# A linear-attention and GEGLU block on one core: 1/den from four copies in DRAM, rows summed beside den, and the down projection's first product of each pair moved up

## The chip, the cores and the metric

The kernel runs on one core of one Trainium2 chip. The metric is the device time of one execution in microseconds (us); the kernel before took 783.16 us (median of three runs, 782.22 to 784.1). The engines of a core run their own instruction streams in order and wait for each other through semaphores: PE (matrix multiply, with PEld for its weight loads), DVE (VectorE), ACT (ScalarE), POOL (GpSimd), and SP, which here only issues DMAs.

## The reference

One sequence of 2048 tokens, D = 1024, 32 heads of 32, F = 3584. Six modulation vectors come from `silu(c) @ w_mod`.

```python
h = _layernorm(x, axis=-1) * (1 + ca) + sa
x = x + ga * _A_ref(h, A_wqkv, A_wo)
h = _layernorm(x, axis=-1) * (1 + cb) + sb
x = x + gb * _B_ref(h, B_w_gate, B_w_up, B_w_down)
# _A_ref: linear attention
pq, pk = (phi(q), phi(k))
kv = jnp.einsum('bhsd,bhse->bhde', pk, v)
z = jnp.einsum('bhsd->bhd', pk)
num = jnp.einsum('bhqd,bhde->bhqe', pq, kv)
den = jnp.einsum('bhqd,bhd->bhq', pq, z)[..., None] + 1e-06
o = num / den          # then o @ wo
# _B_ref: gelu(x @ w_gate) * (x @ w_up) @ w_down
```

## The kernel before

The program is built as one list of operations per engine. Each operation names the bytes that it reads and writes; a tracker derives the semaphore waits. From the first attention evictions to the second FFN unit (`mark[0]` to `mark[1]`) a planner, `reorder`, sorts the operations of DVE, ACT and POOL by table costs and due times; PE and SP keep the order in which the code emits them. Everything later is in the written order on all engines. SP issues its DMAs in order, so a DMA that waits holds those behind it; eight DMA lanes limit how many are open.

**Attention (about 30 to 241 us).** K and Q come first. Then 24 `m` tiles (line 895) form pk-transpose times x, four groups `g` with three column parts `k` first, then the rest. Each is evicted by ACT (`mcp`), and a finished group is transposed by a DMA (`mT0` to `mT7`, line 703) and multiplied with wv (`kv`, line 913), whose masked blocks DVE writes to `kvt`. `w2_pair(i)` (line 1201) multiplies two groups of `kvt` with wo in 64x64 array tiles, copied to `w2` by ACT or DVE. The table `HOOK` says which of these follow which tile on PE:

```python
HOOK = {0: "ga", 6: "kv0", 10: "kv1", 11: "w0", 13: "kv2", 15: "modp kv3 z32", 16: "den0", 17: "w1 rb0.0 rb0.1", 18: "",
        19: "kv4", 20: "den1 ps0.0", 21: "gbr", 22: "ps0.1", 23: "rb2.0"}
```

`den(p)` (line 1240) needs `z32`. It forms the denominators of two of the four 512-token groups in 128x32 array tiles (32 matmuls of 256 columns, four at a time). DVE adds 1e-6 and takes the reciprocal into `rdc`, whose 128 partitions are token group, half, and head within a group. A DMA stores `rdc` to DRAM (`scr_rd`, line 1248). `rb_load` (line 1260) reads it back so that partition 32k to 32k+31 of the tile `rb` hold the row of head k: four DMAs for each half of a token group, each of 32 partitions with one 8 KB row. `pq_scale` (line 1273, `pqs`) multiplies pq by it, four DVE operations for a half, each waiting for all four loads. `wo` chunks (line 1283) then give the attention output, and `x1` (line 1291) adds it to x.

The modulation sums (`macc` on DVE) end in rows that are split in a high and a low part and summed over partitions by `mod_rows` (`modr`, line 840, 128x32 array tiles, 8 matmuls): "ga" behind tile 0, the pass for sb and cb ("modp") behind tile 15, the pass for gb ("gbr") behind tile 21. ACT copies the row (`mrow`), a DMA stores it, and `sbT` and `cbT` (line 1230) load it back, 4 bytes at a time.

**FFN (241 to 603 us).** 28 units; each forms two 128-column blocks of gate and up by a scheme of seven block products P1 to P7 in place of eight. P1 and P2 are in bf16, the other five are of sums and in f32.

**Down projection (from 603 us).** Eight pairs of 128-token chunks, the same seven products of 14 matmuls each (`d_prod`, line 1672); the pairs alternate between PSUM banks 0 to 3 and 4 to 7 (`b0`). P1 goes to bank b0, is copied to b0+2 (`dpcp`, ACT), P2 is added in b0. P5 goes to b0+3 and is copied to the SBUF tile `de` (`descp`, ACT). P6 and P7 are added in b0+2; with `de` DVE makes bank b0+1 after P6 and b0+3 after P7 (`dpadd`). P3 is added in b0+1, P4 in b0+2. Each of the four banks is evicted by two DVE operations (`x2a`, `x2b`, lines 1576 and 1577) with the residual tile `xq` and stored (`out`). A pair's operands are loaded from DRAM in two halves (`ya`, line 1571): half 0 serves P1, half 1 P2; DVE makes the sums `dssum0` to `dssum3` of them (line 1648) in two buffers used in turn, ACT a copy (`dscp`, line 1643). `y_next(r)` asks for the next pair's half r, `x_in` (line 1568) for `xq`. The order in a pair is

```python
for k in (1, 5, 6, 2, 7, 3, 4):
```

## Time and profile before

| | |
|---|---|
| median of three runs | 783.16 us (782.22 to 784.1) |
| profiled execution, span from first to last instruction | 780.9 us (780.946); its own time beside the span is not shown |
| mean granted clock of PE | 1.000 |
| PE busy | 770.2 us, 99% |
| DVE busy | 645.9 us, 83% |
| ACT busy | 374.6 us, 48% |
| loads of `rb` | 32 of 256 KB, median 6.0 us from issue to landing |
| DVE's waits for `rb` | 2.2 us in 2 waits |
| PE, 125 to 241 us / 241 to 603 / 603 to 623 / 623 to 778 | busy 115.58 of 116 / 360.06 of 362 / 19.93 of 20 / 154.28 of 155 |

PE's busy time is modelled: matmuls overlap each other, a 512-column matmul is shown as 379 to 398 ns and the next one starts some 216 to 230 ns after it. So 99% does not mean that PE runs at its peak; the distance from one start to the next is what to read. In the timeline a row is a group of like instructions, with the start, the busy time, and the number after x. "PEld" rows are the weight loads, one for each matmul; "SPq" rows are DMA issues on SP's queue. "128*32" in a PE row is the array tile.

### The profile page before, as it was taken

How to read it: one execution, taken by the hardware profiler on the slowest of the kernel's cores; microseconds unless marked ns; L12 is line 12 of the kernel's file. 1: busy time of each engine (PE TensorE's matmuls, PEld its weight loads, DVE VectorE, ACT ScalarE, POOL GpSimd, SP SyncE). 2: the span in 40 equal slices, each digit the busy share in tenths (PEclk: the TensorE clock that was granted, in tenths of full speed). 3: DMA queues.
4: the chain of work that ended last, by engine and by line, in shares of the span. 5: the costliest groups of instructions: out<-in, count | busy, mean ns of one | idle time of the engine just before them, and what ended most of it. 6: DMA issues, size and time to landing. Idle time of an engine off the chain costs nothing.

```text
span 780.9 us, 10753 instructions
## 1 busy us (share of the span) xinstructions
PE 770.2 (99%) x3825; PEld 496.2 (64%) x3883; DVE 645.9 (83%) x964; ACT 374.6 (48%) x629; POOL 47.5 (6%) x126
## 2 busy tenths in 40 slices
PE   8999999999999999999999999999999999999998
PEld 4444445666445667667676767667676576677766
DVE  6699988897899878787989888888989888676767
ACT  2497743242466487878755555555555211111111
POOL 2031300000321011100000000000000000000000
PEclk9999999999999999999999999999999999999999
DMA  9879749939999358867353865535356334443331
GB/s 284 256 167 252 158 91 215 255 80 196 203 287 231 82 138 212 230 175 215 99 145 108 250 211 172 148 96 161 97 147 221 111 127 139 144 141 114 126 125 60
DMA packets 196940, 130.22 MB, mean 167 GB/s; under 512 B 69516, under 2 KB 182420, under 8 KB 195864
## 3 DMA queue, kind: packets, MB, share of 16 engines
q1 hardware_dynamic: 196872, 129.55, 62.4%
q8 instruction: 30, 0.49, 0.3%
q14 instruction: 22, 0.18, 0.1%
q10 hardware_dynamic: 16, 0.00, 0.0%
HBM read 92.55 MB, written 23.35 MB: 148 GB/s over the span
## 4 chain that ended last, share of the span: by engine, by line
PE 95%; SPq 2%; DMA 1%; DVE 1%; issue 1%; ACT 0%; DVEq 0%; ACTq 0%
PE ps_all L1458 45%; PE ps_all L1672 21%; PE ps_all L895 7%; PE ps_all L934 7%; PE ps_all L1283 7%; PE ps_all L880 5%; PE ps_all L1593 1%; SPq L598 1%; DMA wmq<-in_w_mod_dram 1%; SPq L603 1%; DMA h1T<-xh 0%; PE ps_all L913 0%; PE ps_all L1201 0%; PE ps_all L1240 0%; DVE h1T L724 0%
## 5 line engine op out<-in xcount | busy, mean ns | idle before, releaser
L1458 PE MATMUL ps_all<-ss,tp 128*128 128x512 f32 x896 | 214.3, 396 | 0.0
L1458 PEld LDWEIGHTS ps_all<-ss,tp 128*128 128x128 f32 x896 | 168.3, 188 | 37.8 <-DVE ss L1413 0.2
L1672 PE MATMUL ps_all<-dt,sb 128*128 128x512 f32 x424 | 102.5, 398 | 0.0
L1481 ACT ACTIVATE ge<-ps_all 128x512 f32<-128x512 f32 x112 | 64.1, 597 | 73.8 <-DVE ps_all L1469 62.1
L1458 PE MATMUL ps_all<-h2a,wt 128*128 128x512 bf16 x421 | 95.7, 379 | 1.8
L1672 PEld LDWEIGHTS ps_all<-dt,sb 128*128 128x128 f32 x424 | 79.6, 188 | 18.5 <-DVE sb L1648 0.3
L1476 DVE TENSOR_TENSOR ps_all<-ps_all,es 128x512 f32<-128x512 f32 x54 | 37.6, 699 | 49.4 <-ACT es L1466 49.0
L1488 DVE TENSOR_TENSOR ys<-ge,ps_all 128x512 bf16<-128x512 f32 x112 | 74.4, 684 | 3.8 <-PE ps_all L1672 0.5
L1458 PEld LDWEIGHTS ps_all<-h2a,wt 128*128 128x128 bf16 x448 | 38.0, 98 | 57.3 <-ACT ps_all L1463 16.9
L1433 DVE TENSOR_TENSOR tp<-wt 128x1024 fp32r<-128x1024 bf16 x56 | 68.1, 1217 | 1.8 <-DMA wt<-in_B_w_up_dram 1.8
L1433 DVE TENSOR_TENSOR tp<-wt,tp 128x1024 fp32r<-128x1024 bf16 x56 | 68.2, 1218 | 0.0
L934 PE MATMUL ps_all<-h1T,wq 128*128 128x512 bf16 x256 | 56.7, 379 | 0.0
L880 PE MATMUL ps_all<-wk,h1T 128*128 128x512 bf16 x239 | 55.3, 379 | 1.1 <-DMA wk<-in_A_wqkv_dram 0.5
L1283 PE MATMUL ps_all<-w,pq 128*128 128x512 bf16 x249 | 55.7, 379 | 0.5 <-issue 0.2
L1458 PE MATMUL ps_all<-ar,tp 128*128 128x512 f32 x224 | 55.5, 390 | 0.0
L869 ACT ACTIVATE eb<-ps_all 128x512 f32<-128x512 f32 x64 | 36.3, 594 | 37.6 <-PE ps_all L880 16.0
L1672 PE MATMUL ps_all<-wd,ya 128*128 128x512 bf16 x199 | 47.5, 380 | 0.7
L1458 PEld LDWEIGHTS ps_all<-ar,tp 128*128 128x128 f32 x224 | 42.1, 188 | 8.9
L1463 ACT ACTIVATE ps_all<-ps_all 128x512 f32<-128x512 f32 x56 | 32.6, 582 | 26.8 <-PE ps_all L1458 26.5
L934 PEld LDWEIGHTS ps_all<-h1T,wq 128*128 128x128 bf16 x256 | 25.0, 98 | 30.0
L1283 PEld LDWEIGHTS ps_all<-w,pq 128*128 128x128 bf16 x256 | 24.6, 98 | 30.3 <-issue 1.1
L1643 ACT ACTIVATE sb<-ya 128x896 fp32r<-128x896 bf16 (+1 forms) x16 | 14.5, 913 | 58.8 <-PE ps_all L1672 58.8
(141 smaller groups left out, 976.3 us busy)
## 6 DMA issues: line engine op xcount, KB each, us to landing
wt<-in_B_w_gate_dram SPq DMA_DIRECT2D x28, 512.0 KB, 4.0
wt<-in_B_w_up_dram SPq DMA_DIRECT2D x28, 512.0 KB, 5.2
scr_y<-ys SPq DMA_DIRECT2D x28, 512.0 KB, 3.2
ya<-scr_y SPq DMA_DIRECT2D x14, 896.0 KB, 4.9
rb<-scr_rd SPq DMA_DIRECT2D x32, 256.0 KB, 6.0
wd<-in_B_w_down_dram SPq DMA_DIRECT2D x7, 1024.0 KB, 7.6
wmst<-in_w_mod_dram SPq DMA_DIRECT2D x6, 1024.0 KB, 6.2
wmq<-in_w_mod_dram SPq DMA_DIRECT2D x8, 512.0 KB, 7.5
```

What stands on the lines that cost most here:

```text
L869: sch.op(A, lambda e: e.activation(EB[i][:, :], PS(bank), ACTF.Exp), prd=pr(bank), wr=rng, note=f"{note}.exp")
L880: o = sch.op(T, lambda e, dc=dc: e.matmul(PS(bank), H1[sg][:, ci, dc, :], W_[:, dc, jg * 512:(jg + 1) * 512], start=(dc == 0), stop=(dc == ...
L895: o = sch.op(T, lambda e, c_=c_: e.matmul(PS(bank, 0, n), PK[c_][:, g * P:(g + 1) * P], xrow(c_, o_, o_ + n), start=(c_ == 0), stop=(c_ == ...
L934: o = sch.op(T, lambda e, dc=dc: e.matmul(PS(b), WQ[:, dc, qc * P:(qc + 1) * P], H1[sg][:, :, dc, :], start=(dc == 0), stop=(dc == NDC - 1 ...
L1283: last[half] = sch.op(T, lambda e, g=g, half=half: e.matmul(PS(b0 + half), PQ[sg][:, g, ci * P:(ci + 1) * P], W2[:, g, half * 512:(half + ...
L1433: sch.op(V, lambda e: e.tensor_tensor(TP[k][:], in0, in1 if k in (0, 2) else in1[:], ALU.subtract), rd=r0 + r1, wr=r_tp(k), deps=[x1_ops[7 ...
L1458: o = sch.op(T, lambda e, l_=l_, r_=r_, dc=dc: e.matmul(PS(b), l_, r_, start=fresh and dc == 0, stop=dc == ND2 - 1, skip_group_check=True) ...
L1463: sch.op(A, lambda e: e.activation(PS(BB + t), PS(BA + t), ACTF.Copy), prd=pr(BA + t), pwr=pr(BB + t), note="pcp")
L1476: sch.op(V, lambda e: e.tensor_tensor(PS(BC + t), PS(BC + t), ES[t][:, :], ALU.add), prd=pr(BC + t), rd=r_2k(OFF_ES[t], f"es{t}"), pwr=pr( ...
L1481: sch.op(A, lambda e: e.activation(GE[i][:, :], PS(b), ACTF.Gelu_apprx_tanh), prd=pr(b), wr=r_2k(OFF_GE[i], f"ge{i}"), note="gelu")
L1488: sch.op(V, lambda e: e.tensor_tensor(YS[s_][:, 2 * h:2 * h + 2, t, :], q(GE[i][:, :]), q(PS(b + 1)), ALU.mult), rd=r_2k(OFF_GE[i], f"ge{i ...
L1672: o = sch.op(T, lambda e, l_=l_, r_=r_, j=j, dst=dst: e.matmul(dst, l_[:, 0, :], r_, start=(k in (1, 5) or own is not None) and j == js[0] ...
```

## The change

- `scr_rd` gets four copies (`NRP`), so `rdc` is stored four times. `rb_load` still makes four DMAs for a half, but each now fills two of the eight groups on all 128 partitions, rows of 2 KB; every copy serves eight partitions of a head. A `pqs` operation waits for its own load alone. Two dependencies are put in by hand for the planner: the first `pqs` behind the second reciprocal, `pqs2.0` behind the copy `w2cp7`.
- Hooks: "modp" moves from tile 15 to 16, ahead of `den0`, its bank from 5 to 2; `den0` uses bank 3; `w1` moves from 17 to 16, behind `den0`. The stores of `rdc` become hooks of their own (`st0`, `st1`). "gbr" moves from tile 21 to 20, behind `den1`, into bank 6. `sbT` and `cbT` are loaded behind `st1` ("sbl"). On SP's queue `mT4` now stands ahead of the first store, and `mrow2` and `mT6` ahead of the second.
- Down projection, pairs 1 to 6: the order becomes 5, 6, 7, 2, then P1 of the next pair (`d_open`), 3, 4. P1 of pair 1 is opened before the loop. P7 gets bank b0+3 for itself once P5 has been copied from it; `d_join` copies P7 to `de` and adds it to b0+1 (giving b0+3) and to b0+2. Half 1 of `ya` is asked for behind P2, and the `xq` loads are spread differently. The last pair keeps the old order without its P1.

```diff
-    scr_rd = nc.dram_tensor("scr_rd", [NSG, 2, HPG, NG, SGW // 2], f32).ap()
+    NRP = 4
+    scr_rd = nc.dram_tensor("scr_rd", [NSG, 2, HPG, NRP, NG, SGW // 2], f32).ap()
...
-            mod_rows(((0, 2, 5, lambda j, h: (HLG[:, j, h, :], r_hlg(j, h))),))
+            mod_rows(((0, 2, 6, lambda j, h: (HLG[:, j, h, :], r_hlg(j, h))),))
...
-            mod_rows(((2, 4, 5, hl_src),))
-            o_r = mod_store(4, 5, MROW[1], r_2k(OFF_ROW + 2048, "mrow1"), 1)
+            mod_rows(((2, 4, 2, hl_src),))
+            o_sc[0] = mod_store(4, 2, MROW[1], r_2k(OFF_ROW + 2048, "mrow1"), 1)
+
+        o_sc = [None]
+
+        def mod_load():
             for dst, nt, a0 in ((SBT, "sbT", 0), (CBT, "cbT", 2)):
...
-                o_rd[pr_] = sch.dma(Q, lambda e: e.dma_start(scr_rd[2 * pr_:2 * pr_ + 2].rearrange("s f k g t -> (s f k g) t"), RDC[:, :]),
-                          rd=r_sm("rdc"), note=f"rden{pr_}.st")
+                o_rd[pr_] = [sch.dma(Q, lambda e, r=r: e.dma_start(scr_rd[2 * pr_:2 * pr_ + 2, :, :, r, :, :].rearrange("s f k g t -> (s f k) g t"), RDC[:, :]),
+                                     rd=r_sm("rdc"), note=f"rden{pr_}.st") for r in range(NRP)]
...
-                for k in range(HPG):
-                    made.append(sch.dma(Q, lambda e, h=h, k=k: e.dma_start(
-                        RB[i][32 * k:32 * (k + 1), h, :, :].rearrange("p a b -> p (a b)"),
-                        scr_rd[sg, h, k:k + 1, :, :].rearrange("k g t -> k (g t)").to_broadcast([32, NG * HW])),
-                        wr=r_rb(i, h) if k == 0 else (), deps=made[0].deps if k else [o_rd[sg // 2]], note=f"rb{sg}.{h}.{k}"))
+                for g0 in range(0, NG, 2):
+                    src = scr_rd[sg, h, :, :, g0:g0 + 2, :].rearrange("k r g t -> (k r) (g t)").unsqueeze(1).to_broadcast([HPG * NRP, P // (HPG * NRP), 2 * HW])
+                    sch.dma(Q, lambda e, h=h, g0=g0, src=src: e.dma_start(
+                        RB[i][:, h, g0:g0 + 2, :].rearrange("p a b -> p (a b)"), src),
+                        wr=r_rb(i, h, g0, g0 + 2), deps=o_rd[sg // 2], note=f"rb{sg}.{h}.{g0}")
...
-        HOOK = {0: "ga", 6: "kv0", 10: "kv1", 11: "w0", 13: "kv2", 15: "modp kv3 z32", 16: "den0", 17: "w1 rb0.0 rb0.1", 18: "",
-                19: "kv4", 20: "den1 ps0.0", 21: "gbr", 22: "ps0.1", 23: "rb2.0"}
+        HOOK = {0: "ga", 6: "kv0", 10: "kv1", 11: "w0", 13: "kv2", 15: "kv3 z32", 16: "modp den0 w1", 17: "st0 rb0.0 rb0.1", 18: "",
+                19: "kv4", 20: "den1 gbr ps0.0", 22: "st1 sbl ps0.1", 23: "rb2.0"}
...
-            b = b0 + {1: 0, 2: 0, 5: 3, 6: 2, 7: 2, 4: 2, 3: 1}[k] if own is None else own
+            b = b0 + {1: 0, 2: 0, 5: 3, 6: 2, 7: 3 if 0 < ca < 4 * CPG - 2 else 2, 4: 2, 3: 1}[k] if own is None else own
...
+        def d_join(b0):
+            d_ecp(b0 + 3)
+            d_add(b0 + 3, b0 + 1)
+            d_add(b0 + 2, b0 + 2)
+
+        def d_open(i):
+            b = i % 2 * 4
+            d_prod(2 * i, b, 1)
+            d_cp(b + 2, b, "dpcp")
...
-            for k in (1, 5, 6, 2, 7, 3, 4):
+            for k in ((5, 6, 2, 7, 3, 4) if last else (5, 6, 7, 2, 1, 3, 4)):
...
+                if k == 1:
+                    d_open(i + 1)
+                    hook(k)
+                    continue
...
+                elif k == 7:
+                    if last:
+                        d_add(b0 + 3, b0 + 2)
+                    else:
+                        d_join(b0)
+                    d_s(ca, 4)
+                    evac(*parts[3])
                 elif k == 2:
+                    y_next(1)
                     evac(*parts[0])
...
-                    if k == 1:
-                        x_in(i, 0, 3, 1)
-                    elif k == 5:
-                        x_in(i, 2)
+                    if k == 5:
+                        x_in(i, 1, 2)
...
+                if more and k in (1, 4):
+                    x_in(i + 1, 3 if k == 1 else 0)
...
+        d_open(1)
+        d_t(2, 5)
+        d_t(2, 6)
```

## The prediction

> **What bounds the kernel now.** I read the page's busy times and its chain first, then what the matmul engine (PE) waits for, then its timeline stage by stage, and last the DMA issues around the changed loads.
>
> ```profile
> PE 770.2 (99%) x3825; PEld 496.2 (64%) x3883; DVE 645.9 (83%) x964; ACT 374.6 (48%) x629; POOL 47.5 (6%) x126
> PE 95%; SPq 2%; DMA 1%; DVE 1%; issue 1%; ACT 0%; DVEq 0%; ACTq 0%
> rb<-scr_rd SPq DMA_DIRECT2D x32, 256.0 KB, 6.0
> ```
>
> PE is the bound. The waits of PE from 125 us to the end hold one entry of 0.2 us, so no load of `rb` (1/den) stops PE today. VectorE (DVE) waits for `rb` twice, 2.2 us in all, and PE does not notice. What the change can win has to lie between matmuls that are already back to back. The PE timeline around the first `den`:
>
> ```profile
> 165.69 1.47 PE L895 MATMUL ps_all<-xall,pk 128*128 128x341 bf16 x9
> 167.09 0.61 PE L840 MATMUL ps_all<-hl,ones 128*32 128x512 bf16 x8
> 167.64 0.62 PE L913 MATMUL ps_all<-mtb,wv 128*128 128x128 bf16 x8
> 169.11 1.47 PE L895 MATMUL ps_all<-xall,pk 128*128 128x342 bf16 x9
> 170.51 1.06 PE L1240 MATMUL ps_all<-pq,z 128*32 128x256 bf16 x32
> 171.50 1.19 PE L895 MATMUL ps_all<-xrow,pk 128*128 128x342 bf16 x7
> 172.53 1.47 PE L895 MATMUL ps_all<-xall,pk 128*128 128x342 bf16 x9
> 173.93 0.63 PE L1201 MATMUL ps_all<-wo,kvt 64*64 64x512 bf16 x8
> ```
>
> Columns are start, busy, and the array tile in use. Seven 342-wide matmuls take 1.03 us from 171.50 to 172.53, so 0.146 each. Nine from 169.11 end their turn at 170.42, yet the 128x32 stretch starts at 170.51: 0.09 lost on entering. `den`'s 8 rounds of 4 are 256 wide, half of a 512-wide matmul's 0.216, so 0.87; the next tile starts 0.99 after `den`: 0.12 lost on leaving. The 64x64 stretch loses 0.09 the same way (172.53 + 9 x 0.146 = 173.84). So each change of the array's tiling costs about 0.095.
>
> The weight loads of one down-projection pair:
>
> ```profile
> 664.18 3.13 PEld L1672 LDWEIGHTS ps_all<-dh,sb 128*128 128x128 f32 x14
> 667.58 2.71 PEld L1672 LDWEIGHTS ps_all<-wd,ya 128*128 128x128 bf16 x14 [0.26 <-issue]
> 670.40 6.35 PEld L1672 LDWEIGHTS ps_all<-dt,sb 128*128 128x128 f32 x28
> 677.01 2.70 PEld L1672 LDWEIGHTS ps_all<-wd,ya 128*128 128x128 bf16 x14 [0.26 <-issue]
> 679.84 6.35 PEld L1672 LDWEIGHTS ps_all<-dt,sb 128*128 128x128 f32 x28
> 686.23 3.13 PEld L1672 LDWEIGHTS ps_all<-dh,sb 128*128 128x128 f32 x14
> 689.62 2.27 PEld L1672 LDWEIGHTS ps_all<-wd,ya 128*128 128x128 bf16 x12 [0.26 <-issue]
> ```
>
> A pair takes 22.04 (667.58 to 689.62) for 28 bf16 and 70 f32 products. Pure f32 spacing is (3.13 - 0.19)/13 = 0.226; pure bf16 is 0.216 (121 loads of line 1283 in 26.00 from 209.08). 28 x 0.216 + 70 x 0.2264 = 21.89, so 0.15 goes to two separate bf16 stretches, 0.07 each. An FFN unit has one stretch per 56 products: 12.57 against 12.50, again 0.07.
>
> **The change part by part.**
> *Array order.* P1 of the next pair comes right behind P2, so pairs 1 to 6 have one bf16 stretch instead of two: 6 x 0.07 = 0.42 saved. `modr` of the second pass moves from tile 15 to stand directly ahead of `den0`, and the second `w2` group directly behind it: six tiling changes (two each) become three. The `gb` rows move up to `den1`: four become two. Five changes fewer, 5 x 0.095 = 0.47. The boundary between `den` (128x32) and `w2` (64x64) is not in this trace; its bounds are 0 and 0.12, and I count it as a full change, as every other boundary shows. The Trainium skill says in "TensorEngine Tiling (Array Packing)", section "Key Properties", that a change of tiling mode drains the engine; by it `den` to `w2` costs a switch and `modr` to `den` none, which is the sum as made; if it were free there, 0.09 more would be won.
>
> *Second-order work in the down pair.* P7 gets its own bank; one ACT copy (0.60, the `de` copy's row) and one DVE add (0.70) are added in six pairs. DVE has gaps of 0.9 to 2.2 us between products in this stage and ACT is idle over 7 us, so it costs nothing as long as the new order's deadlines hold. The tight one: between P3's end and P5 of the next pair there was P4 and P1, now only P4, 3.17. By DVE's timeline it starts the P3 eviction 0.42 after P4's first weight load (686.23 to 686.65); the second half of an eviction starts 0.80 after the first (671.26, 672.06), the next `dssum` 0.61 behind that (672.67) and runs 1.08: 2.92 in all. 0.25 is left, and the second half of `dssum0` (1.00 later) is needed only seven products on. Cost taken: 0; bounds 0 and 0.3 per pair. The next `ya` (P1's operand) can be asked for once `dssum2` is done and the `xq` load ahead of it on SP's queue has gone. That `xq` waits for an output: P4's end, two `dssum1` pieces, two eviction pieces and 1.74 for the output to land put the `ya` issue near 9.8 us after P4's first load; `ya` landed 6.0 after issue behind four `xq` loads and 4.6 to 4.8 alone: 14.4 to 15.8. P1 starts at 15.9. Cost 0. The other half of `ya` is asked for right behind P2, no longer behind P7, some 3 us earlier against its use: DVE's wait for it (8.1 us in six) should go, off PE's path.
>
> *The 1/den path.* Stores of `rdc` go from 2 to 8 issues (about 0.45 of SP each), the 32 loads stay 32, with 128 rows of 2 KB instead of 32 of 8 KB. `sbT` and `cbT` move behind the stores of `den1`, `mT4` ahead of those of `den0`. SP issues in order, so what matters is who stands behind the loads:
>
> ```profile
> 174.40 0.81 SPq L1248 DMA_DIRECT2D scr_rd<-rdc  x1
> 175.32 1.27 SPq L703 DMA_TRANSPOSE mtb<-mb  x1
> 176.69 3.76 SPq L1260 DMA_DIRECT2D rb<-scr_rd  x8
> 180.55 1.23 SPq L703 DMA_TRANSPOSE mtb<-mb  x1
> 185.74 0.35 SPq L1248 DMA_DIRECT2D scr_rd<-rdc  x1
> ```
>
> The transpose of 180.55 (`mT5`) takes 9.0 us to land, 189.6, because it queues behind the eight loads (first lands 3.6 after issue, last 8.6: 1.2 apart). PE needs it for `kv5` at 190.42: 0.8 us of cover. After the change `mT4` goes at about 175.1 (its eviction now follows two `w2` copies of 0.97 on ACT, from 172.1, behind an `mhi` of 0.63), the four stores from 176.4 to 177.8, the last lands 2.2 later (the first store's time), 180.0, and only then the loads start, 3.3 later than today. A load that takes x lands first at 180.0 + 2.4 + x (3.6 - 1.2 is the fixed part), the eighth at 182.4 + 8x, `mT5` 0.95 behind it (today's 189.6 against the last load's 188.6). `kv5` is due 0.47 earlier, at about 189.9, so PE starts to wait at x = 0.82. Bounds for x: 0.63 (the 4 KB rows of the `gbb` broadcast to 128 partitions ran at 416 GB/s between 243 and 244.3) and 1.26 (today's loads: 208 GB/s from 179 to 188). Between them 2 KB rows to 128 partitions ran at 358 GB/s (242 to 243), 0.73. I take 0.73, nearest in row size and partitions; then `mT5` lands at 189.2 and nothing waits. The Trainium skill's "SBUF — State Buffer", section "Door 1: The DMA port swizzle (why `[64,N]` ≈ `[32,N]`)", says a transfer is as fast as the number of SBUF ports that its partitions reach, and by its table 32 neighbouring partitions reach half of the ports that 128 reach; by it x would be 0.63, half of today's, and the sum stays as it is, since either x is below 0.82.
>
> `mT7` now stands behind four stores and `sbT`/`cbT` (3.9 to land). These go out by about 189.9, `mT7` still waits for its eviction near 190.7, lands 3.1 later at 193.8 and `kv7` is due near 194.5: cost 0. VectorE then scales earlier (its 1.45 wait for `rb` goes), and what is next on PE is the first `wo` chunk, which did not wait. The planner's other moves on DVE and ACT swap neighbours; `z32` goes back to about 167.9, `den0` needs it at 170.3. Cost 0.
>
> **Sum.** 0.47 + 0.42 = 0.89 off the profiled execution: span 780.95 to 780.06. Only the span of that execution is shown; the median of the runs, 783.16, lies 2.2 above it, so 782.3.
>
> **The rivals.**
> - *The transposes wait (slower).* If the 2 KB rows run at today's rate, x = 1.2: `mT5` lands at 192.9, PE stands 3.0 us at `kv5`, net +2.1: 785.3. It cancels the gain from x = 0.93 and is over 0.2% slower from x = 1.13. For it: more rows, more stores, a late start, 0.8 us of cover today. Against it: every 128-partition row above. Chance 0.11.
> - *The pair's operand comes late.* P5 waits for `dssum0` once per pair: at 0.3 each, 6 x 0.3 = 1.8, net +0.9: 784.1. For it: only 0.25 of room. Against it: DVE is idle ahead of that chain, and its pieces repeat to 0.01 us. Chance 0.10.
> - *The order pays only once.* If f32 and bf16 stretches cost by their number of products and not by their borders, 0.42 is lost: 782.7. FFN's 0.07 per single border speaks against it. Chance 0.14.
> - *More hidden waits go.* The tiling groups from 125 to 241 leave some 0.3 us that I can't place: 781.9. Chance 0.10.
>
> **How the numbers follow.** The forecast has 0.55. The three runs spread 1.9 us, so about 0.2% (1.6 us) is what a measurement can tell from no change. The forecast, -0.9, lies inside it, and run noise of about 0.8 carries a fifth of it past: faster 0.22, same 0.62; slower 0.16 from the transposes, part of the late operand, and noise. The range takes in the forecast with its noise, 780.9, and the late-operand case with some of it, 784.7; the transposes' full price stays outside.
>
> **What would show it.** Right: `modr`, `den` and `w2` stand together in the PE timeline, with one loss of 0.09 ahead and one behind; a steady pair of 21.97; loads of `rb` landing 0.65 to 0.75 apart; PE's waits past 125 us still near nothing. Wrong: a wait of PE on `mtb` near 190, or on `sb` at each P5, or on `ya` at P1.

## The result, and the profile after

The changed kernel takes 786.76 us (median of five executions) against 782.59 us before (median of five, the three of the table above among them); the means stand 1.0044 to 1, 95% interval 1.003 to 1.0057. One execution of the five, the one that was profiled, was disturbed (2062 us, the others 785.76 to 787.04) and is left out of the means, so the profile shown here is of the same kernel run again: 785.88 us, span 784.1.

The page's busy times, the chain that ended last, and the loads of `rb`:

```profile
PE 774.0 (99%) x3883; PEld 497.4 (63%) x3883; DVE 647.6 (83%) x970; ACT 376.7 (48%) x635; POOL 48.7 (6%) x126
PE 95%; DMA 2%; SPq 2%; DVE 0%; issue 0%; DVEq 0%
rb<-scr_rd SPq DMA_DIRECT2D x32, 256.0 KB, 6.1
```

The chain is PE's as before, but DMA has 2% where it had 1%. What PE waited for from 125 us to the end (total, times, longest) is one entry, on the transposed tiles `mtb`, where before there was one of 0.2 us on another line:

```profile
PE ps_all L914 <- DMA mtb<-mb: 4.1, 2, 2.5
```

PE's timeline shows the two places, `kv5` and `kv7`. In the kernel before, `kv5` came at 190.42, and `kv6` and `kv7` in one row:

```profile
190.42 0.61 PE L913 MATMUL ps_all<-mtb,wv 128*128 128x128 bf16 x8
194.57 1.05 PE L913 MATMUL ps_all<-mtb,wv 128*128 128x128 bf16 x16
```

In the changed kernel:

```profile
188.30 1.47 PE L896 MATMUL ps_all<-xall,pk 128*128 128x342 bf16 x9
192.29 0.62 PE L914 MATMUL ps_all<-mtb,wv 128*128 128x128 bf16 x8 [2.52 <-DMA mtb<-mb]
...
196.46 0.61 PE L914 MATMUL ps_all<-mtb,wv 128*128 128x128 bf16 x8
198.61 0.61 PE L914 MATMUL ps_all<-mtb,wv 128*128 128x128 bf16 x8 [1.54 <-DMA mtb<-mb]
```

SP's queue shows what the two transposes stood behind (start, time of issue). Before, `mT6` and `mT7` were issued so:

```profile
186.20 2.16 SPq L703 DMA_TRANSPOSE mtb<-mb  x1
191.15 1.26 SPq L703 DMA_TRANSPOSE mtb<-mb  x1
```

and in the changed kernel the queue is

```profile
174.64 1.25 SPq L704 DMA_TRANSPOSE mtb<-mb  x1
175.95 2.51 SPq L1255 DMA_DIRECT2D scr_rd<-rdc  x4
180.32 5.05 SPq L1267 DMA_DIRECT2D rb<-scr_rd  x8
185.48 1.25 SPq L704 DMA_TRANSPOSE mtb<-mb  x1
186.84 0.73 SPq L850 DMA_DIRECT2D scr_row<-mrg  x1
187.68 3.48 SPq L704 DMA_TRANSPOSE mtb<-mb  x1
191.26 2.49 SPq L1255 DMA_DIRECT2D scr_rd<-rdc  x4
193.79 0.59 SPq L1237 DMA_DIRECT2D sbT<-scr_row  x1
194.43 0.68 SPq L1237 DMA_DIRECT2D cbT<-scr_row  x1
195.22 1.42 SPq L704 DMA_TRANSPOSE mtb<-mb  x1
```

The rows are `mT4`, four stores, eight loads, `mT5`, a row's store, `mT6`, four stores, `sbT`, `cbT`, `mT7`. The first load goes out at 180.32, 3.63 later than before (176.69). Of that 1.92 is three more stores at 0.64 from one to the next; of the remaining 1.71, 1.55 is the stores' new place behind `mT4`, and the rest is a slightly longer way from the last store to the first load. By their records the eight loads land between 183.94 and 191.33, 1.06 apart on average (unevenly: the fourth at 186.82, the fifth at 189.33; before 180.26 to 188.62, 1.19 apart), which gives 0.97 back, and `mT5` lands 0.91 behind the last, at 192.24: 2.66 later than before (189.58). The cover was 0.84 and PE comes 0.80 earlier, so it waits 2.6. `mT7` goes out 4.07 later than before (195.22 against 191.15), since `mT6`'s issue held the queue until 191.16 and four stores, `sbT` and `cbT` stood behind it.

The two gains are there. PE around the first `den`:

```profile
169.59 0.62 PE L841 MATMUL ps_all<-hl,ones 128*32 128x512 bf16 x8
170.04 1.05 PE L1247 MATMUL ps_all<-pq,z 128*32 128x256 bf16 x32
171.01 0.63 PE L1204 MATMUL ps_all<-wo,kvt 64*64 64x512 bf16 x8
171.57 1.19 PE L896 MATMUL ps_all<-xrow,pk 128*128 128x342 bf16 x7
```

`modr`, `den` and `w2` stand together. From `den`'s start to `w2`'s is 0.97 where the matmuls need 0.87: the border from 128x32 to 64x64 costs 0.10, a full change, as the sum had it and as the rule cited there from the Trainium skill ("TensorEngine Tiling (Array Packing)", section "Key Properties") says. One down-projection pair, the weight loads:

```profile
661.61 5.73 PEld L1680 LDWEIGHTS ps_all<-wd,ya 128*128 128x128 bf16 x28 [0.26 <-issue]
667.46 3.17 PEld L1680 LDWEIGHTS ps_all<-dt,sb 128*128 128x128 f32 x14
670.67 3.13 PEld L1680 LDWEIGHTS ps_all<-dh,sb 128*128 128x128 f32 x14
673.85 9.48 PEld L1680 LDWEIGHTS ps_all<-dt,sb 128*128 128x128 f32 x42
683.59 5.73 PEld L1680 LDWEIGHTS ps_all<-wd,ya 128*128 128x128 bf16 x28 [0.26 <-issue]
```

One bf16 stretch of 28 and 21.98 from one to the next, where it was two and 22.04.

Matched by weight loads, the profiled span adds up so: 0.26 earlier before the first `m` tile (the start differs from run to run), 0.54 won by the order up to `kv5`, 4.4 lost at the two waits with what starts slowly behind them, 0.35 won in the down projection, and 0.11 elsewhere, nearly all of it in the FFN, for no reason that the trace shows: 780.95 - 0.26 - 0.54 + 4.4 - 0.35 - 0.11 = 784.1.

### The profile page after: what moved, and what is told of

It reads as the page before. It is cut to its first block, busy times and chain, and to the rows that moved or that the text cites. A ratio compares the mean times of both kernels' runs of the same rounds, so it can differ in the third digit from the quotient of the medians.

```text
span 2060.6 us, 10775 instructions
## 1 busy us (share of the span) xinstructions
PE 2036.0 (99%) x3829; PEld 926.5 (45%) x3883; DVE 665.5 (32%) x970; ACT 390.7 (19%) x635; POOL 43.4 (2%) x126
## 4 chain that ended last, share of the span: by engine, by line
PE 99%; issue 1%; DVE 0%; POOL 0%; ACT 0%; POOLq 0%; ACTq 0%
PE ps_all L1466 45%; PE ps_all L1680 21%; PE ps_all L896 7%; PE ps_all L935 7%; PE ps_all L1288 7%; PE ps_all L881 7%; PE ps_all L1601 1%; PE ps_all L950 1%; PE ps_all L914 0%; PE ps_all L970 0%; PE ps_all L1204 0%; PE ps_all L1247 0%; PE ps_all L695 0%; PE ps_all L767 0%; PE ps_all L841 0%
## 5 line engine op out<-in xcount | busy, mean ns | idle before, releaser
L1466 PE MATMUL ps_all<-ss,tp 128*128 128x512 f32 x896 | 556.1, 846 | 0.0
L1466 PEld LDWEIGHTS ps_all<-ss,tp 128*128 128x128 f32 x896 | 316.3, 353 | 222.8 <-issue 209.6
L1466 PE MATMUL ps_all<-h2a,wt 128*128 128x512 bf16 x421 | 258.1, 837 | 9.6 <-issue 9.6
L1680 PE MATMUL ps_all<-dt,sb 128*128 128x512 f32 x424 | 261.3, 839 | 0.0
L935 PE MATMUL ps_all<-h1T,wq 128*128 128x512 bf16 x256 | 154.1, 835 | 0.0
L1288 PE MATMUL ps_all<-w,pq 128*128 128x512 bf16 x249 | 150.6, 834 | 2.5 <-issue 1.7
L881 PE MATMUL ps_all<-wk,h1T 128*128 128x512 bf16 x239 | 145.8, 830 | 3.6 <-issue 2.8
L1466 PE MATMUL ps_all<-ar,tp 128*128 128x512 f32 x224 | 140.2, 829 | 0.0
L1680 PE MATMUL ps_all<-wd,ya 128*128 128x512 bf16 x203 | 123.8, 838 | 3.0 <-issue 3.0
L896 PE MATMUL ps_all<-xall,pk 128*128 128x342 bf16 (+1 forms) x216 | 91.6, 638 | 0.0
```

Source lines behind the costliest of these rows:

```text
L881: o = sch.op(T, lambda e, dc=dc: e.matmul(PS(bank), H1[sg][:, ci, dc, :], W_[:, dc, jg * 512:(jg + 1) * 512], start=(dc == 0), stop=(dc == ...
L896: o = sch.op(T, lambda e, c_=c_: e.matmul(PS(bank, 0, n), PK[c_][:, g * P:(g + 1) * P], xrow(c_, o_, o_ + n), start=(c_ == 0), stop=(c_ == ...
L935: o = sch.op(T, lambda e, dc=dc: e.matmul(PS(b), WQ[:, dc, qc * P:(qc + 1) * P], H1[sg][:, :, dc, :], start=(dc == 0), stop=(dc == NDC - 1 ...
L1288: last[half] = sch.op(T, lambda e, g=g, half=half: e.matmul(PS(b0 + half), PQ[sg][:, g, ci * P:(ci + 1) * P], W2[:, g, half * 512:(half + ...
L1466: o = sch.op(T, lambda e, l_=l_, r_=r_, dc=dc: e.matmul(PS(b), l_, r_, start=fresh and dc == 0, stop=dc == ND2 - 1, skip_group_check=True) ...
L1680: o = sch.op(T, lambda e, l_=l_, r_=r_, j=j, dst=dst: e.matmul(dst, l_[:, 0, :], r_, start=(k in (1, 5) or k == 7 and 0 < ca < 4 * CPG - 2 ...
```

## The experiments

Edits are against the changed kernel, unless another is named. Times are medians.

**The changed kernel again, and its two halves.** No edit in the first. The second is the kernel before with the down projection's order alone, the third the changed kernel with the old down projection:

```diff
# down projection alone, against the kernel before
-            for k in (1, 5, 6, 2, 7, 3, 4):
+            for k in ((5, 6, 2, 7, 3, 4) if last else (5, 6, 7, 2, 1, 3, 4)):
...
# attention alone, against the changed kernel
-            for k in ((5, 6, 2, 7, 3, 4) if last else (5, 6, 7, 2, 1, 3, 4)):
+            for k in (1, 5, 6, 2, 7, 3, 4):
...
```

> The changed kernel once more, for a profile of it. It took some 3 to 4 us more than before, where 0.9 less was forecast, so about 4 to 5 us of new waiting must stand somewhere. Theory A, the transposes wait: the timeline of PE has one gap of 3 to 5 us near 190 us, before the line that multiplies wv with the transposed tile, and a pair of the down projection takes 21.97 us. Theory B, the pair's operand comes late: nothing near 190 us, and a pair takes 22.5 to 22.7 us instead of 22.04, a wait of PE on sb or ya in each of six pairs. Theory C, PE's granted clock is lower with the new order: no gap, matmuls farther apart in many stages.

> Only the down projection's new order, all else as before. Theory A: 0.4 us faster than before, 782.2. Theory B: slower by all that the change lost, 3 to 4 us, near 786. Theory C: slower by a part of it, with a granted clock under 1.000.

> The down projection as before, all the rest changed (four copies of 1/den, the hooks). Theory A: slower by 3 to 4 us, near 786. Theory B: 0.5 us faster than before, 782.1. Theory C: between the two.

Measured: 786.51 us (ratio 1.0045, 1.003 to 1.006), 782.19 (0.9997, 0.9988 to 1.0007) and 786.68 (1.0049, 1.0034 to 1.0064). The whole loss is the attention part's. The down projection alone has no PE wait past 125 us, and four of the five distances between its doubled bf16 stretches are 21.97 or 21.98; what its median wins, 0.4 us, is less than the start of a run scatters.

The attention part's profile shows a second price. In its windows (stretch, length and PE's busy time first; the third number from the end is the granted clock) PE stands idle from 190 to 194 and then runs at half its clock:

```profile
185.00:190.00 5.00, 4.98 (x35) 3.10 (x32) 3.67 (x7) 0.91 (x2) 0.00 (x0) 1.00 1.21 267
190.00:194.00 4.00, 0.30 (x6) 0.30 (x7) 2.02 (x3) 0.46 (x1) 0.00 (x0) 1.00 1.03 143
194.00:197.50 3.50, 3.50 (x14) 1.32 (x11) 0.45 (x2) 0.00 (x0) 0.00 (x0) 0.51 0.76 149
197.50:205.00 7.50, 7.50 (x58) 3.40 (x58) 4.96 (x9) 2.05 (x2) 0.00 (x0) 1.00 0.84 218
```

3.4 us at half the clock are 1.7 us lost on top of the wait. The execution of the changed kernel that is shown above has no such stretch; its other three had mean clocks of 0.996 to 0.998 (spans 784.2 to 785.4), while 18 of the 19 of the kernel before had 1.000.

**The copies alone.** The kernel before, with four copies and 2 KB rows, the old hooks:

```diff
# against the kernel before
+    NRP = 4
...
-                o_rd[pr_] = sch.dma(Q, lambda e: e.dma_start(scr_rd[2 * pr_:2 * pr_ + 2].rearrange("s f k g t -> (s f k g) t"), RDC[:, :]),
+                o_rd[pr_] = [sch.dma(Q, lambda e, r=r: e.dma_start(scr_rd[2 * pr_:2 * pr_ + 2, :, :, r, :, :].rearrange("s f k g t -> (s f k) g t"), RDC[:, :]),
...
```

> Only the four copies of 1/den in DRAM with loads of 128 rows of 2 KB; hooks and down projection as before. The first store stands ahead of mT4 here. Theory A, if the loads or stores themselves are slow: mT5 lands after 190 us and PE waits there, 2 to 3 us slower than before. If only the new place of the stores behind mT4 is to blame: within 0.5 us of before. Theory B: within 0.3 us of before. The distance between landings of two rb loads says whether 0.73 us was right (as forecast) or 1.2 us.

Measured: 784.02 us (1.0021, 1.0011 to 1.003). The stores stand ahead of `mT4` here:

```profile
174.31 2.54 SPq L1249 DMA_DIRECT2D scr_rd<-rdc  x4
176.96 1.32 SPq L704 DMA_TRANSPOSE mtb<-mb  x1
178.84 5.05 SPq L1260 DMA_DIRECT2D rb<-scr_rd  x8
```

`mT4` goes out at 176.96 in place of 175.32 and lands at 180.18, and `kv4`, which needs it, starts at 180.27 after a wait of 1.0 us (the profile gives no engine for it); PE then waits no more. Both figures of theory A miss, the 2 to 3 us as well as the 0.5. The loads land 0.98 apart (the second at 183.79, the eighth at 189.66), neither 0.73 nor 1.2. So the copies cost wherever they stand: ahead of `mT4` they hold it, behind it they hold the loads and `mT5`.

**`mT5` first.** The second half of the first eight loads moves behind `mT5`:

```diff
-17: "st0 rb0.0 rb0.1", 18: "", 19: "kv4",
+17: "st0 rb0.0", 18: "", 19: "kv4 rb0.1",
```

> The changed kernel, with the four loads of the second half (rb0.1) moved behind mT5 on SP's queue; the four copies, the 2 KB rows and the late first store stay. Theory queue (mT5 is late because it stands behind eight loads, and mT6's issue, the stores and mT7 are late in turn): the 2.5 us at kv5 go; mT6 no longer holds SP, so the 1.6 at kv7 shrink to under 0.6; in all 3.5 to 4 us less than the changed kernel, 782 to 783, span near 780.5. Theory extra traffic (the additional stores and slower rows cost wherever they stand): the wait moves to kv6, kv7 or the first wo chunk, and over 2 us of loss remain, 784.5 or more.

Measured: 787.38 us (1.006, 1.004 to 1.008), no gain. `kv5` no longer waits (`mT5` lands at 189.11), but `kv6` and `kv7` do:

```profile
195.41 0.62 PE L914 MATMUL ps_all<-mtb,wv 128*128 128x128 bf16 x8 [0.74 <-DMA mtb<-mb]
199.20 1.01 PE L914 MATMUL ps_all<-mtb,wv 128*128 128x128 bf16 x8 [3.17 <-DMA mtb<-mb]
```

`mT7` was issued at 195.13, as late as in the changed kernel (195.22): it stood behind the second four stores, `sbT` and `cbT` all the same. So `mT7` is late whatever `mT5` does. In the changed kernel the wait at `kv5` had paid for most of that lateness beforehand; with that wait gone, all of it falls on `kv6` and `kv7`. Behind the 3.17 the clock was at 0.52 from 198.5 to 205.5.

**One copy.** Store and loads as before, the rest as changed; once with the store where the change has it, behind `mT4`, once directly behind its reciprocal:

```diff
# both
-                                     rd=r_sm("rdc"), note=f"rden{pr_}.st") for r in range(NRP)]
+                          rd=r_sm("rdc"), note=f"rden{pr_}.st")
...
# the second
-16: "modp den0 w1", 17: "st0 rb0.0 rb0.1", ... 20: "den1 gbr ps0.0", 22: "st1 sbl ps0.1"
+16: "modp den0 st0 w1", 17: "rb0.0 rb0.1", ... 20: "den1 st1 gbr ps0.0", 22: "sbl ps0.1"
```

> The changed kernel with 1/den as before: one store, 32 loads of 8 KB rows on 32 partitions; hooks, the store's place behind mT4 and the down projection stay changed. If the place of the store alone is to blame: the store goes at 176 (before: 174.4), loads start 1.6 us later than before, mT5 lands near 191.2 against 189.8 due: a wait of 1.4 at kv5, net 0.4 us slower than before, 783. If the four copies are to blame: no wait of PE, 0.9 faster than before, 781.7.

> As the run before, and the one store directly behind its reciprocal, ahead of mT4, as it was. What stays of the change: the modulation rows and w2 beside den, sbT and cbT behind the second store, and the down projection's order. Both theories: no wait of PE on a transposed tile, 0.9 us faster than before, span 780.0, 781.7. A wait of over 0.3 us at kv5 or kv7 would say that merging the rows itself brings PE there too early.

Measured: 785.94 us (1.0044, 1.0028 to 1.0061) and 783.01 (0.9997, 0.9988 to 1.0007). SP's queue in the first:

```profile
175.04 1.26 SPq L703 DMA_TRANSPOSE mtb<-mb  x1
176.35 0.57 SPq L1254 DMA_DIRECT2D scr_rd<-rdc  x1
178.37 3.59 SPq L1267 DMA_DIRECT2D rb<-scr_rd  x8
182.06 1.25 SPq L703 DMA_TRANSPOSE mtb<-mb  x1
```

Its first load goes out at 178.37, 1.68 later than before: that is the place behind `mT4` alone, and PE waits 2.2 us at `kv5`. (`mT5` landed 2.2 behind the last load there, 0.95 before; why isn't shown.) With the store ahead of `mT4` the first load goes out at 175.57 and no transpose is late. Counted from the start of `den`, so that the scatter of the start falls out, the first load goes out after 6.2 us before, 5.9 with one copy ahead of `mT4`, 7.9 with one copy behind it, 8.4 with four copies at the old place, and 10.3 in the changed kernel. The place thus costs 1.7 to 2.1 on the queue and the copies 2.2 to 2.4.

In time the two don't add up. The place alone costs nearly the whole loss: 785.94 against 783.01, while the changed kernel takes 786.5. There the copies add almost nothing at `kv5`, where PE waits 2.5 with them and 2.2 without: the eight loads take 1.0 less in all, and `mT5` lands 0.9 behind the last of them in place of 2.2. Nor is this all queue: in the first of the two runs the DMA engines moved only 6 GB/s from 190.9 to 192.0, between the last load and the landing of `mT5`. The kernel before has such a lull too (31 GB/s from 189.6 to 190.9), but behind the landing of its `mT5`. What makes it is not shown.

But 0.9 was expected of the second, and its median shows nothing. Up to `kv7` its profile is 0.92 ahead of before's (0.60 of it from the start, 0.32 from the order); then, in the chunks of the output projection (c0 is the first), it is 4.07 from the start of c3 to that of c4 in place of 3.45, with a wait ahead of c4:

```profile
206.40 9.89 PE L1290 MATMUL ps_all<-w,pq 128*128 128x512 bf16 x45 [0.24 <-DVE pq L1280]
```

This is taken up below. In the profiled execution PE still starts its last matmul 0.74 earlier than before; that its span is 0.9 longer comes from the last two output stores, which took 3.3 to 3.6 us to land in place of 1.7.

The order wins only 0.32 here and not 0.54, and the trace shows why: DVE finishes the low part of the `gb` rows at 182.24, when PE is already in their product (line 840), which takes 0.62 in place of the 0.39 of the changed kernel. That is 0.23.

**Distinct rows.** The loads of `rb` read 128 different rows of `w_gate` in place of the copies, so the scale is not 1/den and what is computed from it is not the reference's:

```diff
-src = scr_rd[sg, h, :, :, g0:g0 + 2, :].rearrange("k r g t -> (k r) (g t)").unsqueeze(1).to_broadcast([HPG * NRP, P // (HPG * NRP), 2 * HW])
+src = wg_v[:, g0 // 2, (2 * (sg % 2) + h) * 512:(2 * (sg % 2) + h) * 512 + 1024]
```

> The changed kernel, whose rb loads read rows of w_gate, another 2 KB row for each partition, in place of a row of 1/den for eight partitions (the scale of pq is then not 1/den; stores and waits stay). If a row that is read eight times makes a load slow: landings some 0.70 to 0.75 us apart where SP is not the limit, in place of 0.80 to 1.06, and less waiting at kv5. If not: the same distances as in the changed kernel, and the waits at kv5 and kv7 stay within 0.5 us.

Measured: 785.15 us in one run, waits on `mtb` of 3.1 in two, the longest 2.3. The issues are 0.47 apart rather than 0.64, the landings 0.93 rather than 1.06 (183.33 to 189.85). So a row that is read eight times costs SP 0.17 for each issue. That it slows the landings isn't shown by one profile of each, since the same loads land 0.98 to 1.20 apart in other profiles here. Even distinct rows are not at the 0.73 of the forecast, and the wait stays: `mT5` lands at 192.34, as in the changed kernel, though the last load landed 1.5 earlier. Here too the DMA engines are nearly idle in between (6 GB/s from 190.5 to 191.5).

**One replica.** The change's rows over 128 partitions, from a single copy; again once with the hooks as changed and once with the store directly behind its reciprocal:

```diff
-    NRP = 4
+    NRP = 1
```

> The changed kernel with one replica in place of four (NRP = 1): one store per half, and the same 2 KB rows over 128 partitions, each group of 32 partitions now reading one 2 KB row. The hooks, the order of the modulation rows and the down projection stay as changed. Theory A (SP's issue of the stores, 0.64 us each, starts the loads late, and a load takes its 1.06 us whatever it reads from): three stores fewer start the first load 3 x 0.64 = 1.92 us earlier, near 178.4, mT5 lands near 190.3 rather than 192.24, kv5 (due 189.8) waits 0.5 us rather than 2.5, and kv7 as little; PE waits of 0.5 to 1.5 us on the transposes in all, median 783.0 to 784.0. Theory B (32 partitions that read one row collide, and the copies are what keeps a load at 1.06 us): landings 1.2 us or more apart, mT5 at 191.5 or later, waits of 2.5 us and more, median 785.5 to 787.

> One replica and 2 KB rows as in the run before, and each store directly behind its reciprocal, ahead of mT4 and of the next modulation rows (den0 st0 w1; den1 st1 gbr). Theory A: no wait on a transpose, first load issued near 175.6, eight loads in 7.4 us, mT5 near 187.5. With 32-partition loads in this order 0.6 us was lost again at the output projection's product c3 (4.07 us in place of 3.45), where a scaled quotient came late behind loads 1.2 us apart; at 1.06 us apart that loss goes, and the order's gain stays: span near 780.0, median 781.8 (781.3 to 782.6). Theory B (row collisions): loads 1.2 us or more apart, the loss at c3 stays or grows, 783 to 784.

Measured: 833.11 us (1.0645, 1.0627 to 1.0663) and 832.23 (1.063, 1.0614 to 1.0646), far outside both theories. PE waits 13.6 us for a transpose and 15.0 for quotients. The share that packets took of 16 engines, first between 184 and 191 us in the changed kernel:

```profile
q1 hardware_dynamic: 1325, 1.64, 94.7%
```

and then between 182 and 190 us with one replica:

```profile
q1 hardware_dynamic: 375, 0.74, 25.3%
```

A quarter, four engines of 16, and 2.5 us from one load's issue to the next. The source of such a load has four rows as its outermost dimension, in the changed kernel 16. The Trainium skill, "DMA: Bandwidth & Descriptors", section "Why a DMA increments its semaphore by 16 and not by 1", says that the number of engines is the largest up to 16 that divides the slowest dimension on both sides; by it one copy gets 4 and four copies 16, and the trace agrees (25% and 95%). So the four copies are what buys the 2 KB rows their engines.

**Transposes first.** All copies and rows as changed; `mT5` ahead of the second four loads, `mT6` and `mT7` ahead of the second four stores:

```diff
-17: "st0 rb0.0 rb0.1", ... 19: "kv4", 20: "den1 gbr ps0.0", 22: "st1 sbl ps0.1", 23: "rb2.0"
+17: "st0 rb0.0", ... 19: "kv4 rb0.1", 20: "den1 gbr ps0.0", 22: "ps0.1", 23: "st1 sbl rb2.0"
```

> The changed kernel with all four copies, but in SP's queue mT5 stands ahead of the second four loads and mT6 and mT7 ahead of the second four stores, sbT and cbT. Theory A (only the place in the queue makes the transposes late): kv5 does not wait, kv6 waits 0.7 us at most behind the loads that are in flight, kv7 under 1 us; the stores of the second half go out 1 to 2 us earlier or later than in the changed kernel, and the quotients of rb2 and rb1 become the next thing that is late, at the output projection's product c3, by 0 to 2 us: median 783 to 785. Theory B (the copies' traffic on the DMA engines makes the transposes late wherever they stand): waits of 3 to 4 us on the transposes remain, 786 to 787.5. Where PE has idled for over 2 us the granted clock may fall to 0.5 for some microseconds, as it did in three runs here, which adds 1.7 us or more.

Measured: 783.82 us (1.0016, 1.0007 to 1.0026). PE's waits past 100 us:

```profile
PE ps_all L1288 <- DVE pq L1278: 0.8, 1, 0.8
PE ps_all L914 <- DMA mtb<-mb: 0.5, 2, 0.3
PE ps_all L1680 <- DMA ya<-scr_y: 0.4, 1, 0.4
```

With every copy, row and byte kept, the wait for the transposes falls from 4.1 to 0.5. The place in SP's queue makes them late (theory A). What comes next is the quotient ahead of c4 (DVE's product of pq and 1/den).

**A hybrid.** One copy and old loads for the first half, four copies and new loads for the second:

```diff
-                                     rd=r_sm("rdc"), note=f"rden{pr_}.st") for r in range(NRP)]
+                                     rd=r_sm("rdc"), note=f"rden{pr_}.st") for r in range(NRP if pr_ else 1)]
...
```

> The changed kernel, with the first half as before (one store, directly behind its reciprocal and ahead of mT4; loads of 8 KB rows over 32 partitions), and the second half as changed (four copies, 2 KB rows over 128 partitions, on 16 engines), its stores directly behind their reciprocal. The run with one copy for both halves, in the same order, had no wait on a transpose, was 0.9 us ahead of before's stages up to kv7, and lost 0.4 to 0.6 us of it at the product c3 (4.07 us for 3.45). Theory A (c3's loss is the loads of the second half, 1.2 us apart): with them 0.95 us apart c3 takes 3.45 us, no PE wait after 100 us, the span is 780.0 (780.95 less 0.95) and the median 781.8 (781.3 to 782.3). Theory B (four store issues in a row, 2.6 us of SP, make mT6 or mT7 late wherever they stand): a wait of 0.5 to 2 us on mtb, median 782.5 to 784. Theory C (the new order loses 0.4 us at the projection whatever the loads do): no wait on mtb, c3 and c4 together over 7.2 us, median 782.5 to 783.1.

Measured: 783.49 us (1.0004, 0.9995 to 1.0013). A wait of 0.3 on `mtb`, and 1.0 ahead of c4. Theory B's wait is there but smaller than it said, and theory A is wrong on c4, which needs a quotient of sg 1 (the second token group): its loads belong to the first half and stood behind the new loads of sg 2 and four stores.

**Stores on ACT's queue.** Three of the four stores of a half are issued by ACT, with four DMA lanes for it; once with the hooks as changed, once with SP's store directly behind its reciprocal:

```diff
-    LANES = {SP_: 8, POOL_: 4, ACT_: 2}
+    LANES = {SP_: 8, POOL_: 4, ACT_: 4}
...
-                o_rd[pr_] = [sch.dma(Q, lambda e, r=r: ...
+                o_rd[pr_] = [sch.dma(A if r else Q, lambda e, r=r: ...
```

> The changed kernel with three of the four stores of each half issued by ACT in place of SP. Copies, 2 KB rows, order and down projection stay as changed. Theory A (SP's issue time of the stores makes the transposes late): the first load goes out near 178.4 rather than 180.32, mT5 lands near 190.3 (192.24 in the changed kernel), and mT7, with three stores fewer ahead of it, near 195; PE waits 0.5 to 1.2 us on the transposes in place of 4.1, median 782.8 to 783.5. Theory B (the copies' traffic and the 2 KB rows make them late): the waits stay at 3 us or more, median 785.5 to 787. ACT's own copies come up to 1.9 us later, which costs nothing while ACT idles 1.9 us ahead of each of them.

> As the run before, and the store that SP keeps stands directly behind its reciprocal, ahead of mT4 (den0 st0 w1) and of the next modulation rows (den1 st1 gbr). Theory A: first load near 177.5, mT5 near 189.4, kv5 waits 0.2 us at most, kv7 none, c4 does not wait since rb2's first quotients need one 2 KB load and not four: span 780.0 to 780.4, median 781.8 to 782.2, the first version to show the order's 0.5 and the down projection's 0.4 us together. Theory B: waits of 2 us and more on mtb, median 784 to 786. Theory C (the order's gain is lost at c4 however the loads come): no wait on mtb, 0.3 to 0.6 us more ahead of c4, median 782.3 to 782.8.

Measured: 787.11 us (1.006, 1.0045 to 1.0074) and 786.54 (1.0044, 1.0031 to 1.0058). Theory A misses: PE waits 4.0 and 3.5 us for a transpose. SP's queue in the second:

```profile
174.39 0.58 SPq L1255 DMA_DIRECT2D scr_rd<-rdc  x1
175.07 1.33 SPq L704 DMA_TRANSPOSE mtb<-mb  x1
179.65 5.05 SPq L1267 DMA_DIRECT2D rb<-scr_rd  x8
184.79 1.26 SPq L704 DMA_TRANSPOSE mtb<-mb  x1
```

SP is free at 176.4, but the first load waits for the last copy until 179.65; `mT4` takes 4.3 us to land (4.0 in the first of the two runs), where it took 3.0 to 3.2 in every profile with all stores on SP, and `mT5` lands at 194.04, 3.4 behind the last load (190.61). With all stores on SP that distance was 0.9 to 1.0 in most profiles, but 2.2 and 2.5 with one copy behind `mT4` and with distinct rows. So a transpose that has stores from ACT's queue beside it lands later here, by a mechanism that these runs don't show, and SP's issue time isn't all that the stores cost.

**The quotient that c4 needs, first.** One copy, store behind its reciprocal (the run of 783.01 above), and sg 1's first loads and quotients ahead of sg 2's; beside it the down projection alone again:

```diff
# against the kernel with one copy, store behind its reciprocal
-22: "sbl ps0.1", 23: "rb2.0"}
+22: "sbl ps0.1", 23: "rb1.0"}
...
-        rb_load(1)
-        rb_load(2, (1,))
+        rb_load(1, (1,))
+        rb_load(2)
...
-        pq_scale(2, 0, GH[0] + GH[1])
+        pq_scale(1, 0, GH[0] + GH[1])
...
-        SLOT = {2: lambda: (pq_scale(1, 0, GH[0] + GH[1]), x_dma(NXR, 10)),
+        SLOT = {2: lambda: x_dma(NXR, 10),
...
-                4: lambda: (cb1(), wt_dma(0)),
+                4: lambda: (cb1(), wt_dma(0), pq_scale(2, 0, GH[0] + GH[1])),
```

> One copy for both halves, each store directly behind its reciprocal, old loads, changed order and down projection (as the run of that name that had no wait on a transpose), and in addition the first half of sg 1 (rb1.0 and its quotients) ahead of that of sg 2 on SP and VectorE, since c4 needs the one and only c8 the other. Theory A (c4's start is set by VectorE's order, in which two quotients of sg 2 stand between x1 and the first quotient of sg 1): c4 follows c3 without a wait, c3 to c4 takes 3.45 us and not 4.07, no PE wait after 100 us; span near 780.0 (780.95 less 0.95), median 781.8 (781.3 to 782.2). Theory B (the tiling order's gain is not there, or is lost elsewhere): median 782.3 to 783.0, with waits elsewhere or longer stretches without a wait.

> The down projection's order alone, again, on the same chip as the run before. By the forecast's own step 0.42 us less than before: span 780.5, median 0.4 us under that of the kernel before; the tiling order's 0.47 us should then be the distance between this run and the one with the quotients first, if Theory A of that run holds; under Theory B the two agree or this one is the faster.

Measured: 782.18 us (781.58 to 782.99; ratio 0.9992, 0.9983 to 1.0001) and 783.01 (1.0002, 0.9993 to 1.0011). Theory A: the first has no PE wait past 125 us, and PE goes from c1 through c4 without a break (start, busy):

```profile
196.16 20.03 PE L1290 MATMUL ps_all<-w,pq 128*128 128x512 bf16 x92
```

VectorE's timeline shows why c4 stood. In the kernel with one copy, first, and before, second:

```profile
204.46 3.70 DVE L1280 TENSOR_TENSOR pq<-pq,rb 128x512 bf16<-128x512 bf16 x6
```

```profile
205.38 3.09 DVE L1273 TENSOR_TENSOR pq<-pq,rb 128x512 bf16<-128x512 bf16 x5
```

The planner put two quotients of sg 2 ahead of sg 1's first there, one before. Each takes 0.6 from start to start, so the third ends at 206.35 where c4 was due at 205.8; before, the second ended at 206.67 and c4 began at 206.72. The kernel before was just in time at a second place beside `kv5`. This version keeps 0.32 of the tiling order (its `gb` rows take 0.62 as well) and 0.31 of the down projection, measured from the first `m` tile on; its ratio is the lowest of all, but the interval still reaches 1, so that it is faster is not shown. The down projection alone came out at 0.4 under before's median the first time and 0.3 over it the second. Its two profiles reach the first `m` tile 0.48 earlier and 1.08 later than before's: the start scatters by more than the gain. In the second PE waited 0.3 for a `ya`, and that pair took 22.40, which used up the gain of the stage.

## Why the prediction was wrong

It forecast 782.3 with a range up to 784.7; the kernel takes 786.5 to 786.8. What happened is the rival "the transposes wait", which had a chance of 0.11.

- *The array order, 0.47 and 0.42: right in kind.* 0.54 and 0.35 in the profile above, 0.32 and 0.31 in the version without waits. The pair went to 21.98 (21.97 forecast), but only four distances are that short and not six; the first is still 22.04. The border from `den` to `w2` cost a full change.
- *The 1/den path: the step that failed is x = 0.73.* It was taken from one microsecond, 242 to 243, of the load of `xall`, whose 2 KB rows are all different. That load's 512 KB ran from 241.35 to 243.12, which is 0.88 for 256 KB over its whole length and so above the step's own break-even of 0.82. The loads of `rb` landed 1.06 apart, inside the step's bounds (0.63 to 1.26). The step's formula, with 1.06, puts `mT5` at 182.4 + 8.5 + 0.95 = 191.8; 192.24 was measured. That a smaller x alone would have saved `kv5` is not shown: with distinct rows (0.93) and with one copy behind `mT4` the last load landed 1.5 and 1.2 earlier and `mT5` no earlier, so the fixed 0.95 behind the last load does not always hold either. The stores were put at 0.45 of SP each and took 0.64, yet their landing (180.0) was off by only 0.2, since the first went out 0.45 earlier than forecast (175.95 for 176.4); that is luck. The rule cited there from the Trainium skill ("SBUF — State Buffer", section "Door 1: The DMA port swizzle (why `[64,N]` ≈ `[32,N]`)") would have had 0.63; the trace does not agree, since 256 KB to 128 partitions took 1.06 and to 32 partitions 1.19.
- *`mT7`, cost 0: wrong.* The step had stores, `sbT` and `cbT` out by 189.9. The issue of `mT6` held SP until 191.16, 0.2 before the last load landed, and they went out from 191.26 to 195.1. This cost 1.6 beyond `kv5`'s wait, and the run with `mT5` first shows that it alone would have cost nearly the whole.
- *The rival's price was too low.* With x = 1.2 it had 3.0 us at `kv5` and 785.3. `kv5` waited 2.5; it lacked `kv7`, and the halved clock that shows in part of the executions (spans 0.1 to 1.3 us longer than the one shown).
- *Late operands, d_join, `ya`: right at 0 in the changed kernel.* PE waits for neither `sb` nor `ya`. In two of the experiments it waits 0.3 to 0.4 for one `ya`, and the down projection then wins nothing, so the room there is thin.
- *"What is next on PE is the first `wo` chunk, which did not wait": wrong where the transposes are in time.* c4 had 0.05 of room on VectorE's order; the changed kernel doesn't show it, because PE is 3.6 late there.

The price of a load was carried over from the fastest microsecond of another load. The break-even lay inside the bounds that were given with it, and the rival's chance followed the one row and not the bounds. The 2.2 between the span and the median came from three executions; from all five the median before is 782.59, and the same sum would have given 781.7.

## What to carry to other kernels

A transfer that takes little time itself still costs its issue (0.64 us here) and its place in an in-order queue: before a transfer is made several, list who stands behind it on that queue and how much cover each has, to the last one and not only the first. Moving one transfer behind another can cost as much as adding some: here the place of one store was worth more than three extra stores. A rate is read over the whole of a transfer. Where a kernel is at 99% on one engine, several waits are often just covered; a gain of 0.5 us meets the next of them (`kv5`, `kv7`, c4 here) and is only kept if each is moved as well. A wait on PE may cost more than its length, because the clock can fall behind it.

## What the runs showed of the hardware

- PE's granted clock fell to 0.5 for 3.41 us behind a wait of 3.7 us (the attention part alone) and of 2.2 (one copy behind `mT4`), and for 6.83 us behind one of 3.2 (`mT5` first); behind waits of 2.5 and 1.5 in the profile shown above it stayed at 1.00. In the run with `mT5` first, the windows are:

```profile
195.00:198.50 3.50, 0.62 (x8) 0.45 (x8) 1.63 (x5) 0.00 (x0) 0.00 (x0) 0.98 1.08 199
198.50:205.50 7.00, 6.30 (x27) 2.47 (x28) 2.89 (x6) 1.02 (x1) 0.00 (x0) 0.52 0.79 236
```

  Where a wait falls counts as well as its length. Every full stretch of the clock in the traces is a multiple of 3.41 us. In the slots of 3.41 us that these stretches mark off, PE was busy for 0.30, 1.21 and 0.62 us in the slot just ahead of the three falls, while the 2.5 us in the profile above are spread over two slots (1.53 and 2.78 us busy). Of all slots at full clock in the 17 profiles, the clock fell behind each of the 16 with up to 1.32 us busy and behind none with 1.67 or more; of three between 1.50 and 1.56 it fell behind one. This fits that only some executions of the same kernel have the slow stretch.

  The Trainium skill, "TensorE: Matmul & The Clock Gate", section "Part 1: The HAM clock gate (the "warmup" mystery)", has a free-running window of 3.4 us, half the clock after an idle window and the full one after a busy window. Lengths of 3.41 and 6.83 agree with one and two windows; a fall behind a slot with 1.21 us of busy time does not fit a window that must be idle throughout.
- The share of the DMA engines that a load gets follows its access pattern: the same 256 KB took 1.06 us at 95% with 16 rows outermost in the source, and 2.5 at 25% with four.
- The issue of one DMA took 0.42 us for 32 rows of 8 KB, 0.60 for 128 rows of 2 KB that are read eight times, and 0.43 for 128 distinct rows.
- The issue of `mT6` took 3.5 us of SP in the changed kernel and 2.2 before (`mT4` 1.25). In the nine profiles where it took 1.9 us or more behind eight loads in a row (the runs with one replica aside), it ended between 0.34 us ahead of the landing of the last of them and 0.08 behind it, whenever it had begun. That SP was held by the loads in flight is a likely reading, but with `mT5` ahead of the second four loads it took 2.05 and ended 4.1 ahead of the last landing. No run takes it apart.
